# Loading the V cache of a two-layer decode kernel in transfers of four slots

## The chip, the cores and the metric

The kernel runs on one core of one Trainium2 chip. The metric is the device time in microseconds; each number of the result is a median over several executions. One further execution was recorded by the hardware profiler, and all durations of single operations come from it.

## The reference

Eight sequences (B = 8) of one new token each go through two identical layers: attention over a cache, then a small dense network, each behind a layernorm and added to its input. Both layers read the same K and V caches.

```python
# B=8, D=512, Hq=32, Hkv=8, Sk=8192, Dh=128, F=1792; bf16
def A(x, k_cache, v_cache, wq, wo):          # caches: (B, Hkv, Sk, Dh)
    q = (x @ wq).reshape(B, 1, Hq, Dh).transpose(0, 2, 1, 3)
    k, v = repeat(k_cache, 4, axis=1), repeat(v_cache, 4, axis=1)
    p = softmax(einsum("bhqd,bhkd->bhqk", q, k) * Dh ** -0.5)
    o = einsum("bhqk,bhkd->bhqd", p, v)
    return o.transpose(0, 2, 1, 3).reshape(B, 1, Hq * Dh) @ wo

def Bnet(x, w1, w2):
    return silu(x @ w1) @ w2

for _ in range(2):
    x = x + A(layernorm(x), A_k_cache, A_v_cache, A_wq, A_wo)
    x = x + Bnet(layernorm(x), B_w1, B_w2)
```

A head's K is 8192 rows of 128 numbers, 2 MB, and its V as much. There are 64 pairs of batch and head.

## The kernel before

**Tasks and steps.** A task is one (layer, batch, KV head) with its four query heads; there are 128. A task has four steps (`SPT`), one for each piece of 2048 keys. A piece of K or V is 512 KB: 128 partitions of 4 KB, that is 16 chunks of 128 keys. Step c transposes its piece of K on TensorE (line 551; eight chunks at a time), ScalarE and VectorE copy the transposes back over the piece (lines 560 and 562), and TensorE multiplies them with the queries (line 585). The softmax of a task follows when its four steps are through, and the product with V (line 645) runs `LAG` = 6 steps behind: step c works on the V of step c - 6.

**Slots.** All pieces live in one tile, `arena`, of `NSLOT` = 28 neighbouring slots of 4 KB per partition. A slot is used again and again; each has a semaphore of its own, which a load into it raises when it has landed.

**Kept heads.** Layer 1 reads the same caches as layer 0. Of heads 3 to 7 the transposed K of layer 0 stays in its slots until layer 1 of the same batch has used it (`KEEP` = 20 pieces, one of them parked in PSUM), and three pieces of head 7's V as well (`KEEPV`). The other heads are loaded again for layer 1. `make_tasks` orders the tasks accordingly: for each batch, layer 0's heads 3 to 7, while the kept K fills slot after slot; then four other tasks, whose loads have to do with the few slots left (called a tight passage here); then layer 1's heads 3 to 7, which load V alone and set the kept slots free; and then other tasks with slots to spare, in layer 0 or 1. The dense network and the queries of layer 1 are computed in between, in small parts, by `chain_of`.

**The plan of the loads.** `lay_loads` writes down before the kernel runs which load goes into which slot. Time is counted in half steps. Each wanted piece has a `need` (the half step of its first use) and a `free` (that of its last). The pieces are sorted by need and taken one by one; a piece goes into the slot that is free first. A piece with an even number takes its right-hand neighbour along, in one load of 1 MB into two neighbouring slots, if the later of the two is free `WIDE` = 8 half steps before the need; the second piece then leaves the list. `after` is the half step after which the load may be issued: the last use of what the slots held. SP issues the loads in the order of the list; at half step 2c or 2c + 1 `issue_until` issues all at the head of the list whose `after` has come, and before each `Sync.acquire` (waits on line 88, issues on line 407) makes SP wait for the instruction that last used the slots.

**Layout.** A load of two pieces reads one contiguous run of 8 KB for each partition, so partition p holds other keys than it would with two single loads. K and V of the same keys, in either layer where they meet, must be laid out alike. `plan_loads` sees to it: where some of a pair of pieces (`rows_of`: layer, batch, head and number of the pair) come as a pair and some as singles, all are made single and the plan is laid again. `issue` reads the cache in the layout that the plan has settled on.

Of the kernel before, what the change touches and what calls it, by code (L numbers as in the profile page):

```python
# [15 lines left out]
SPT = 4  # L16
NSLOT = 28
# [4 lines left out]
LAG = 6  # L22
WIDE = 8
AHEAD = 8
LEAD = 1
NTP = 2
NSCP = 2
# [111 lines left out]
def make_tasks(nb, nkv, keep_from):  # L139


    first = int(keep_from)
    a = [[(0, b, g) for g in range(first)] for b in range(nb)]
    kept = [[(0, b, g) for g in range(first, nkv)] for b in range(nb)]
    c = [[(1, b, g) for g in range(first, nkv)] for b in range(nb)]
    d = [[(1, b, g) for g in range(first)] for b in range(nb)]
    ahead = [t for b in range(1, nb) for t in a[b]]
    behind = []
    tasks = a[0] + kept[0]
    na = 0  # L150
    rest = 2 * len(ahead) - nb * WINDOW

    def put(size, must):
        nonlocal na, tasks
        nd = max(0, min(len(behind), size - max(0, must - na)))
        tasks += behind[:nd]
        del behind[:nd]
        tasks += ahead[na:na + size - nd]
        na += len(ahead[na:na + size - nd])

    for b in range(nb):
        if b:
            tasks += kept[b]
        gap = rest * (b + 1) // (nb - 1) - rest * b // (nb - 1) if b + 1 < nb else 0
        due = first * min(b + 1, nb - 1)
        put(WINDOW if b + 1 < nb else len(behind), due - gap)
        tasks += c[b]
        behind += d[b]
        if b + 1 < nb:
            put(gap, due)  # L170
    tasks += behind
    assert na == len(ahead)
    return tasks


def rows_of(d, kept):
    return 0 if (d.g, d.k) in kept else d.layer, d.b, d.g, d.k // 2


def plan_loads(tasks, kept, parked, keptv, nslot, ngran):  # L180

    single = set()
    while True:
        loads, copies = lay_loads(tasks, kept, parked, keptv, nslot, ngran, single)
        double = {rows_of(d, kept) for d in loads if d.n == 2}
        torn = {rows_of(d, kept) for d in loads if d.n == 1} & double
        if not torn:
            return loads, copies, double
        single |= torn


def closing_from(tasks, kept):

    i = len(tasks)
    while tasks[i - 1][0] == 1 and (tasks[i - 1][2], 0) not in kept:
        i -= 1
    return i * SPT


def lay_loads(tasks, kept, parked, keptv, nslot, ngran, single):  # L200

    at = {t: i for i, t in enumerate(tasks)}
    wanted = []
    late = closing_from(tasks, kept)
    for i, (layer, b, g) in enumerate(tasks):
        for k in range(ngran):
            c = i * SPT + k
            if layer == 0 or (g, k) not in kept:
                last = i if layer or (g, k) not in kept - parked else at[(1, b, g)]
                wanted.append(Load("K", layer, b, g, k, -1 if c < AHEAD else 2 * (c - LEAD if c >= late else c), 2 * (last * SPT + k) + 1))  # L210
            elif (g, k) in parked:
                wanted.append(Load("C", layer, b, g, k, 2 * (c - 1), 2 * c + 1))
            if layer == 0 or (g, k) not in keptv:
                last = i if layer or (g, k) not in keptv else at[(1, b, g)]
                wanted.append(Load("V", layer, b, g, k, 2 * (c + LAG), 2 * (last * SPT + k + LAG)))
    wanted.sort(key=lambda d: (d.need, d.kind))
    free = [-2] * nslot
    loads, copies = [], []
    while wanted:
        d = wanted.pop(0)  # L220
        if d.kind == "C":
            d.slot = max((j for j in range(nslot) if free[j] < d.need - 1), key=lambda j: (free[j], j))
            free[d.slot] = d.free
            copies.append(d)
            continue
        mate = None
        if d.k % 2 == 0 and rows_of(d, kept) not in single:
            same = [e for e in wanted if (e.kind, e.layer, e.b, e.g, e.k) == (d.kind, d.layer, d.b, d.g, d.k + 1)]
            mate = same[0] if same else None
            s = min(range(nslot - 1), key=lambda j: (max(free[j], free[j + 1]), j))  # L230
            after = max(free[s], free[s + 1])
            if after > d.need - WIDE or d.need < 0 or len(wanted) == 1:
                mate = None
        if mate:
            wanted.remove(mate)
            d.n, d.slot, d.after = 2, s, after
            free[s], free[s + 1] = d.free, mate.free
        else:
            d.slot = min(range(nslot), key=lambda j: (free[j], j))
            d.after = free[d.slot]  # L240
            free[d.slot] = d.free
        assert d.after < d.need or d.need == -1 and d.after == -2, (d.kind, d.need, d.after)
        loads.append(d)
    return loads, copies
# [18 lines left out]
def _build(ctx, nc, A_x, A_k_cache, A_v_cache, A_wq, A_wo, B_w1, B_w2, out):  # L263
    B, _sq, D = A_x.shape
    _b, HKV, S, _dh = A_k_cache.shape
# [6 lines left out]
    NGRAN = NCH // (GRP * HALVES)  # L272
# [4 lines left out]
    kept = set(order[len(order) - KEEP:])  # L277
    keptv = set(order[len(order) - KEEPV:])
    tasks = make_tasks(B, HKV, (len(order) - KEEP) // NGRAN)
    assert len(tasks) == 2 * B * HKV  # L280
    task_at = {t: i for i, t in enumerate(tasks)}
    parked = set(order[len(order) - PARK:])
    loads, copies, wide = plan_loads(tasks, kept, parked, keptv, NSLOT, NGRAN)
    NC = len(tasks) * SPT

    pe = nc.tensor
# [103 lines left out]
    def r_half(slot, h):  # L390
        return res(f"slot{slot}_{h}")
# [10 lines left out]
    def dma(eng, out_ap, in_ap, counter, reads=(), writes=()):  # L402
        reads = [res(n) if isinstance(n, str) else n for n in reads]
        writes = [res(n) if isinstance(n, str) else n for n in writes]
        syn.acquire(eng, reads, writes)
        tok = counter.next_tok()
        eng.dma_start(out_ap, in_ap).then_inc(counter.sem, 16)  # L407
        syn.release(tok, reads, writes)
        return tok
# [14 lines left out]

    def issue(d):
        cache = A_k_cache if d.kind == "K" else A_v_cache
        if rows_of(d, kept) in wide:
            src = cache[d.b, d.g].rearrange("(j p i c) d -> p j i (c d)", j=NGRAN // 2, p=128, i=2)
            src = src[:, d.k // 2, d.k % 2:d.k % 2 + d.n].rearrange("p i e -> p (i e)")
        else:  # L430
            src = cache[d.b, d.g].rearrange("(k p c) d -> k p (c d)", k=NGRAN, p=128)[d.k]
        dst = ARENA[:, d.slot * SLOT:(d.slot + d.n) * SLOT]
        dma(sp, dst, src, slsem[d.slot],
            writes=[r_half(s, h) for s in range(d.slot, d.slot + d.n) for h in range(HALVES)])
        for i in range(d.n):
            (k_slot if d.kind == "K" else v_slot)[(d.b, d.g, d.k + i)] = d.slot + i

    with nc.Block() as block:

        @block.sync  # L440
        def _(sync_eng):
# [34 lines left out]
            def issue_until(pos):  # L476
                while queue and queue[0].after <= pos:
                    issue(queue.pop(0))
# [17 lines left out]

            for _n in range(AHEAD):
                issue(queue.pop(0))
# [70 lines left out]
            def emit_q(ti):  # L569
                layer, b, g = tasks[ti]  # L570
                if layer == 0:
                    q, rq = QA[:, b, g * REP:(g + 1) * REP], f"QA{b}"
                else:
                    q, rq = QT2[b % 2][:, g * REP:(g + 1) * REP], f"QT2_{b % 2}"
                qb = QB[ti % NQB][:, NGRAN - 1:NGRAN - 1 + REP * NGRAN:NGRAN]
                op(act, lambda: act.copy(qb, q), reads=[rq], writes=[f"QB{ti % NQB}"])
# [359 lines left out]
            for f in ln_stages(XT[0], "XT0", B, opens):  # L936
# [3 lines left out]
               reads=["PT", "yr"], writes=["PT"])  # L940
            for c in range(AHEAD):
                for h in range(HALVES):
# [32 lines left out]
            def scores(c):  # L975
                layer, _b, g, _k = where(c)
                if not step(TILE) and not chain and turn[0] < B and heads[turn[0]] and layer == 0 and g >= first:
                    add_heads(turn[0])
                emit_s(c)

            for c in range(NC + LAG):
                if c < NC:
                    layer, b, g, k = where(c)
                if c and c % SPT == 0 and c < NC:
                    assert layer == 0 or asked[b] >= (g + 1) * REP
                    emit_q(c // SPT)
                ready = c < NC and (c < AHEAD or layer == 1 and (g, k) in kept)
                if ready:
                    scores(c)
                t = c + LEAD if c >= late - LEAD else c  # L990
                if not ready or t >= late:
# [72 lines left out]
```

## Time and profile before

| | |
|---|---|
| median of 3 runs | 1133.17 us (1130.16 to 1137.92) |
| profiled execution | 1138.0 us, of which the span from the first to the last instruction 1136.2 us |
| TensorE: matmuls busy / weight loads busy | 930.5 us (82%) / 699.6 us (62%) |
| VectorE / ScalarE / GpSimd busy | 555.3 / 492.2 / 117.8 us |
| mean granted TensorE clock | 0.933 of full speed |
| read from memory | 452.47 MB, 398 GB/s over the span |
| loads of K and V | 347 of V (141 of two slots), 268 of K (84 of two slots) |
| chain that ended last | DMA 49%, TensorE 33%, VectorE 8%, ScalarE 4% |

The page of the profile divides the span into 40 equal slices of 28.4 us; a digit is the busy share of a slice in tenths, PEclk the clock that was granted to TensorE, GB/s what the 16 DMA engines moved. DMA queue q1 carries the loads that SP issues, q8 the fetching of instructions. In the waits, "SPq L88 <- PE OTp L645" reads: SP's queue, at line 88, waited for TensorE's matmuls of line 645. "PEld" is TensorE's loading of weights, which for line 645 are chunks of V. Three numbers behind a wait are its sum in microseconds, how often, and the longest. In the list of DMA issues the last number is the median time from the issue to the landing, with all that stood ahead of it in the queue.

### The profile page before, as it was taken

How to read it: one execution, taken by the hardware profiler on the slowest of the kernel's cores; microseconds unless marked ns; L12 is line 12 of the kernel's file. 1: busy time of each engine (PE TensorE's matmuls, PEld its weight loads, DVE VectorE, ACT ScalarE, POOL GpSimd, SP SyncE). 2: the span in 40 equal slices, each digit the busy share in tenths (PEclk: the TensorE clock that was granted, in tenths of full speed). 3: DMA queues.
4: the chain of work that ended last, by engine and by line, in shares of the span. 5: the costliest groups of instructions: out<-in, count | busy, mean ns of one | idle time of the engine just before them, and what ended most of it. 6: DMA issues, size and time to landing. Idle time of an engine off the chain costs nothing.

```text
span 1136.2 us, 42713 instructions
## 1 busy us (share of the span) xinstructions
PE 930.5 (82%) x18792; PEld 699.6 (62%) x18792; DVE 555.3 (49%) x1710; ACT 492.2 (43%) x778; POOL 117.8 (10%) x300
## 2 busy tenths in 40 slices
PE   6687888888888788888888888888888887878886
PEld 4366656666576556666566655666566665766565
DVE  6444554456344544446444554445444463445544
ACT  5354424554255424554245433554245442544332
POOL 0000110011100110001100111001100111001100
PEclk9699988999899988999699998999899997999987
DMA  9999999999999999999999999999999999999995
GB/s 377 416 414 414 393 406 419 417 396 404 416 418 412 334 400 419 417 409 383 399 419 412 387 399 420 418 412 397 407 418 414 398 401 413 418 413 376 400 418 221
DMA packets 91805, 455.25 MB, mean 401 GB/s; under 512 B 10204, under 2 KB 10468, under 8 KB 62308
## 3 DMA queue, kind: packets, MB, share of 16 engines
q1 hardware_dynamic: 91604, 452.51, 98.9%
q8 instruction: 148, 2.42, 0.9%
q14 instruction: 37, 0.30, 0.1%
q10 hardware_dynamic: 16, 0.01, 0.0%
HBM read 452.47 MB, written 0.01 MB: 398 GB/s over the span
## 4 chain that ended last, share of the span: by engine, by line
DMA 49%; PE 33%; DVE 8%; ACT 4%; issue 4%; SPq 2%; POOL 0%; POOLq 0%; ACTq 0%; DVEq 0%
DMA arena<-in_A_v_cache_dram 29%; DMA arena<-in_A_k_cache_dram 18%; PE TPp L551 15%; PE SCp L585 8%; DVE arena L562 7%; PE OTp L645 4%; ACT arena L560 3%; PE MISC L760 3%; DMA wq<-in_A_wq_dram 2%; PE TPp L625 2%; SPq L407 2%; ACT P L609 1%; PE KEPTp L551 1%; DVE small L634 0%; PE MISC L732 0%
## 5 line engine op out<-in xcount | busy, mean ns | idle before, releaser
L560 ACT COPY arena<-TPp 128x1024 bf16<-128x1024 bf16 x344 | 348.3, 1013 | 388.8 <-PE TPp L551 385.6
L562 DVE COPY arena<-TPp 128x1024 bf16<-128x1024 bf16 x344 | 238.0, 692 | 335.7 <-PE TPp L551 333.7
L551 PE MATMUL TPp<-ident,arena 128*128 128x128 bf16 x5504 | 378.8, 223 | 25.9 <-DMA arena<-in_A_k_cache_dram 19.5
L551 PEld LDWEIGHTS TPp<-ident,arena 128*128 128x128 bf16 x5504 | 318.4, 100 | 112.5 <-issue 64.2
L645 PE MATMUL OTp<-PT,arena 128*128 128x32 bf16 x8192 | 291.3, 179 | 59.4 <-DMA arena<-in_A_v_cache_dram 54.1
L645 PEld LDWEIGHTS OTp<-PT,arena 128*128 128x128 bf16 x8192 | 251.9, 97 | 133.7 <-DMA arena<-in_A_v_cache_dram 100.7
L585 PE MATMUL SCp<-arena,QB 128*32 128x512 bf16 x2048 | 221.5, 421 | 73.0 <-DVE arena L562 27.2
L609 ACT ACTIVATE P<-SCp,small 128x512 bf16<-128x512 f32 x128 | 88.0, 688 | 205.6 <-DVE small L607 169.3
L596 DVE TENSOR_REDUCE small<-SCp 128x1 f32<-128x512 f32 x128 | 88.4, 691 | 96.2 <-PE SCp L585 95.0
L585 PEld LDWEIGHTS SCp<-arena,QB 128*32 128x32 bf16 x2048 | 60.3, 95 | 115.5 <-ACT arena L560 52.1
L600 POOL PARTITION_ALL_REDUCE small<-small x128 | 47.7, 373 | 576.9 <-DVE small L598 576.9
L617 POOL PARTITION_ALL_REDUCE small<-small x128 | 55.4, 433 | 327.4 <-DVE at L659 147.9
L625 PE MATMUL TPp<-ident,P 128*128 128x128 bf16 x512 | 55.0, 235 | 30.4 <-ACT arena L560 17.4
L625 PEld LDWEIGHTS TPp<-ident,P 128*128 128x128 bf16 x512 | 31.4, 103 | 40.1 <-ACT arena L560 24.1
L629 DVE COPY PT<-TPp 128x256 bf16<-128x256 bf16 x128 | 37.3, 291 | 21.6 <-PE TPp L625 19.9
L615 DVE TENSOR_SCALAR small<-small 128x4 f32<-128x4 f32 x128 | 28.7, 224 | 31.1 <-ACT P L609 30.8
L598 DVE TENSOR_SCALAR small<-small 128x4 f32<-128x4 f32 x128 | 29.4, 230 | 4.5
L773 DVE STREAM_TRANSPOSE MISC<-MISC 128x128 f32<-128x128 f32 (+2 forms) x40 | 22.0, 550 | 18.0 <-PE MISC L760 18.0
L605 DVE TENSOR_TENSOR small<-small 128x4 f32<-128x4 f32 x128 | 20.0, 156 | 20.9 <-POOL small L600 20.9
L609 ACT ACTIVATION_READ_ACCUMULATOR P<-SCp,small 128x1 f32 x128 | 24.7, 193 | 0.0
L760 PE MATMUL MISC<-wo,at 128*32 128x128 bf16 x1024 | 24.6, 221 | 0.0
L560 ACT COPY arena<-KEPTp 128x1024 bf16<-128x1024 bf16 x16 | 16.2, 1012 | 14.3 <-PE KEPTp L551 10.9
(102 smaller groups left out, 331.6 us busy)
## 6 DMA issues: line engine op xcount, KB each, us to landing
arena<-in_A_v_cache_dram SPq DMA_DIRECT2D x141, 1024.0 KB, 19.6
arena<-in_A_v_cache_dram SPq DMA_DIRECT2D x206, 512.0 KB, 7.0
arena<-in_A_k_cache_dram SPq DMA_DIRECT2D x184, 512.0 KB, 9.4
arena<-in_A_k_cache_dram SPq DMA_DIRECT2D x84, 1024.0 KB, 22.0
arena<-in_A_wo_dram SPq DMA_DIRECT2D x8, 512.0 KB, 12.7
wq<-in_A_wq_dram SPq DMA_DIRECT2D x1, 4096.0 KB, 25.3
w<-in_B_w_dram SPq DMA_DIRECT2D x1, 1792.0 KB, 23.3
arena<-in_B_w_dram SPq DMA_DIRECT2D x3, 512.0 KB, 17.3
```

The costliest lines, as they stand in the source:

```text
L551: lambda c=c: pe.transpose(tpv[:, c, :], chunk(slot, h * GRP + c), ident[:, :])
L560: op(act, lambda: act.copy(dst, bank[:, :]), reads=[rt], writes=[r_half(slot, h)])
L562: op(dve, lambda: dve.tensor_copy(dst, bank[:, :]), reads=[rt], writes=[r_half(slot, h)])
L585: lambda t=t: pe.matmul(SCp[bank][t * QR:(t + 1) * QR, :], QB[qn][:, NGRAN - 1 - k:NGRAN - 1 - k + QR], keys[:, t * KB:(t + 1) * KB], star ...
L596: op(dve, lambda: dve.tensor_reduce(mxp[st][:, :], SCp[bank][:, :], AX.X, ALU.max), reads=[f"SC{bank}"], writes=[f"mxp{st}"])
L600: op(pool, lambda: pool.partition_all_reduce(mxa[st][:, :], mxr[st][:, :], 128, bass.bass_isa.ReduceOp.max), reads=[f"mxr{st}"], writes=[f ...
L609: op(act, lambda: act.activation(P[:, :], SCp[bank][:, :], ACT.Exp, bias=nb[st][:, 0:1], scale=SM_SCALE, accum_out=rs[st][:, :]), reads=[f ...
L617: op(pool, lambda: pool.partition_all_reduce(ssa[st][:, :], ssm[st][:, :], 128, bass.bass_isa.ReduceOp.add), reads=[f"ssm{st}"], writes=[f ...
L625: lambda c=c: pe.transpose(tpv[:, c, :], P[:, c * 128:(c + 1) * 128], ident[:, :])
L629: op(dve, lambda: dve.tensor_copy(PT[:, :, :, :], tpv.rearrange("p c (t q) -> p c t q", q=QR)[:, :, :, 0:NGRAN * REP]), reads=[f"TP{tb}"], ...
L645: lambda n=n, cc=cc: pe.matmul(otp, chunk(slot, n), PT[:, cc % CPB, (cc // CPB) % NT, cc // (CPB * NT)::NGRAN].unsqueeze(2).to_broadcast([ ...
L760: lambda t=t, col=col, w=w, start=start, stop=stop: pe.matmul(MISC[t * QR:(t + 1) * QR, 0:math.prod(w.shape[1:])], spread(col), w, start=s ...
```

## The change

A load of V may now fill four neighbouring slots, all four pieces of a head, in one transfer of 2 MB. It is made where four neighbouring slots are free 16 half steps before the need and where the need doesn't fall into the 18 half steps (nine steps, `CALM`) before the end of a layer-0 task of head 7, behind which the tight passage begins (`entries`, `calm`). K still comes in ones or twos. A load of four reads 16 KB in one run for each partition; K of the same rows is then read in that layout too, in pairs of 8 KB out of each 16. Where a single load falls among rows that are joined in twos or fours, `plan_loads` bars that joining and lays the plan again (`barred` takes the place of `single`, `joined` that of `wide`). The plan comes to 585 loads of K and V.

```diff
+CALM = 9
...
-def rows_of(d, kept):
-    return 0 if (d.g, d.k) in kept else d.layer, d.b, d.g, d.k // 2
+def rows_of(d, kept, n):
+    return n, 0 if (d.g, d.k) in kept else d.layer, d.b, d.g, d.k // n
...
-    single = set()
+    barred = set()
     while True:
-        loads, copies = lay_loads(tasks, kept, parked, keptv, nslot, ngran, single)
-        double = {rows_of(d, kept) for d in loads if d.n == 2}
-        torn = {rows_of(d, kept) for d in loads if d.n == 1} & double
+        loads, copies = lay_loads(tasks, kept, parked, keptv, nslot, ngran, barred)
+        torn = set()
+        joined = {rows_of(d, kept, d.n) for d in loads}
+        for d in loads:
+            for n in (2, 4):
+                if d.n == 1 and rows_of(d, kept, n) in joined:
+                    torn.add(rows_of(d, kept, n))
         if not torn:
-            return loads, copies, double
-        single |= torn
+            return loads, copies, joined
+        barred |= torn
...
+    entries = [2 * SPT * (i + 1) for i, (layer, _b, g) in enumerate(tasks) if layer == 0 and g == max(g for g, _k in kept)]
+
+    def calm(need):
+        return all(not 0 < e - need < 2 * CALM for e in entries)
+
...
-        mate = None
-        if d.k % 2 == 0 and rows_of(d, kept) not in single:
-            same = [e for e in wanted if (e.kind, e.layer, e.b, e.g, e.k) == (d.kind, d.layer, d.b, d.g, d.k + 1)]
-            mate = same[0] if same else None
-            s = min(range(nslot - 1), key=lambda j: (max(free[j], free[j + 1]), j))
-            after = max(free[s], free[s + 1])
-            if after > d.need - WIDE or d.need < 0 or len(wanted) == 1:
-                mate = None
-        if mate:
-            wanted.remove(mate)
-            d.n, d.slot, d.after = 2, s, after
-            free[s], free[s + 1] = d.free, mate.free
-        else:
-            d.slot = min(range(nslot), key=lambda j: (free[j], j))
-            d.after = free[d.slot]
-            free[d.slot] = d.free
+        for n, ahead in ((4, 2 * WIDE), (2, WIDE), (1, 0)):
+            if d.k % n or n > 1 and (rows_of(d, kept, n) in barred or d.need < 0) or n > 2 and (d.kind == "K" or not calm(d.need)):
+                continue
+            mates = [d] + [e for e in wanted if (e.kind, e.layer, e.b, e.g) == (d.kind, d.layer, d.b, d.g) and d.k < e.k < d.k + n]
+            s = min(range(nslot - n + 1), key=lambda j: (max(free[j:j + n]), j))
+            after = max(free[s:s + n])
+            if len(mates) == n and (n == 1 or after <= d.need - ahead and len(wanted) >= n):
+                break
+        d.n, d.slot, d.after = n, s, after
+        for i, e in enumerate(mates):
+            free[s + i] = e.free
+            if i:
+                wanted.remove(e)
...
-        if rows_of(d, kept) in wide:
-            src = cache[d.b, d.g].rearrange("(j p i c) d -> p j i (c d)", j=NGRAN // 2, p=128, i=2)
-            src = src[:, d.k // 2, d.k % 2:d.k % 2 + d.n].rearrange("p i e -> p (i e)")
-        else:
-            src = cache[d.b, d.g].rearrange("(k p c) d -> k p (c d)", k=NGRAN, p=128)[d.k]
+        n = max(n for n in (1, 2, 4) if n == 1 or rows_of(d, kept, n) in joined)
+        src = cache[d.b, d.g].rearrange("(j p i c) d -> j p i (c d)", j=NGRAN // n, p=128, i=n)
+        src = src[d.k // n, :, d.k % n:d.k % n + d.n].rearrange("p i e -> p (i e)")
```

## The prediction

> **What bounds the kernel now.** I read the page first, for the share of the DMA engines and the rate in 40 slices.
>
> ```profile
> span 1136.2 us, 42713 instructions
> ...
> PEclk9699988999899988999699998999899997999987
> DMA  9999999999999999999999999999999999999995
> GB/s 377 416 414 414 393 406 419 417 396 404 416 418 412 334 400 419 417 409 383 399 419 412 387 399 420 418 412 397 407 418 414 398 401 413 418 413 376 400 418 221
> ...
> q1 hardware_dynamic: 91604, 452.51, 98.9%
> q8 instruction: 148, 2.42, 0.9%
> ```
>
> The queue of the loads keeps all 16 DMA engines busy for 98.9% of the span. The rate is not flat: about 418 GB/s in some slices, 376 to 400 in others, 334 once. So I asked for the busy time of single stretches: two in which pairs of slots are loaded (191.7 and 979.8), one in which single slots are loaded (229.0), and two around a tight passage behind kept heads (247.2, 382.7). After the engines, a row has the granted clock, the DMA share and GB/s.
>
> ```profile
> 191.70:219.60 27.90, 23.43 (x496) 19.20 (x496) 13.51 (x37) 14.79 (x21) 2.41 (x6) 1.00 1.01 420
> 229.00:247.00 18.00, 15.13 (x312) 12.44 (x308) 8.69 (x23) 9.79 (x14) 1.61 (x4) 1.00 1.02 408
> 247.20:268.10 20.90, 17.86 (x404) 13.84 (x404) 12.48 (x44) 10.04 (x15) 2.81 (x7) 1.00 1.00 384
> 382.70:397.10 14.40, 10.67 (x224) 7.92 (x224) 6.91 (x26) 5.11 (x8) 1.21 (x3) 0.88 0.90 300
> 979.80:1005.00 25.20, 21.46 (x450) 17.10 (x448) 11.91 (x32) 12.72 (x18) 2.04 (x5) 1.00 1.01 417
> ```
>
> Pairs flow at 420 (or 417), singles at 408, and only the tight passages fall below that. The DMA issues on the page say how deep the queue is:
>
> ```profile
> arena<-in_A_v_cache_dram SPq DMA_DIRECT2D x141, 1024.0 KB, 19.6
> arena<-in_A_v_cache_dram SPq DMA_DIRECT2D x206, 512.0 KB, 7.0
> arena<-in_A_k_cache_dram SPq DMA_DIRECT2D x184, 512.0 KB, 9.4
> arena<-in_A_k_cache_dram SPq DMA_DIRECT2D x84, 1024.0 KB, 22.0
> ```
>
> A pair lands some 20 us after its issue although it moves in 2.5: eight transfers' worth stand ahead of it. A single V lands after 7.0, so the reserve in the tight passages is five transfers. Last come the waits of SP and, for 707 to 745, those of TensorE:
>
> ```profile
> SPq L88 <- PE OTp L645: 426.1, 232, 6.8
> SPq L88 <- PE SCp L585: 138.2, 142, 6.9
> ```
> ```profile
> PEld OTp L645 <- DMA arena<-in_A_v_cache_dram: 2.0, 2, 1.2
> ```
>
> SP waits for slots that TensorE has yet to free, with the DMA queue still full behind it; TensorE meets V that is not there twice in 38 us. Both run nearly level: the bytes set the time, and V lands just before it is used.
>
> **What the change does to the plan.** I worked the new rule through the list of wanted pieces. It gives 585 loads of K and V: V 21 fours, 105 pairs and 194 singles, K 87 pairs and 178 singles. Before it was V 141 and 206, K 84 and 184, together 615. So 18 singles and 33 pairs go and 21 fours come, with the same bytes. Only 21 heads get a four: K must come in pairs there, four adjacent slots must be free 8 steps ahead, and the nine steps before the end of a head-7 task are barred. Single loads shift between the batches' head 6, which accounts for the 18.
>
> **Price of the transfers.** A single of 0.524 MB at 408 GB/s takes 1.285 us, a pair of 1.049 MB at 420 takes 2.497. With a fixed part f and v for each 0.524 MB, f + v = 1.285 and f + 2v = 2.497, so v = 1.212 and f = 0.073. No row shows a four; by the same two terms it takes 0.073 + 4 x 1.212 = 4.921 us. Sum: -18 x 1.285 - 33 x 2.497 + 21 x 4.921 = -2.19 us, that is 30 transfers fewer at 0.073. The bounds from the nearest rows: a four without any fixed part (4.848) makes it -3.7, a four at four singles (5.140) makes it +2.4. I keep 4.921, since rows of 4 KB to 8 KB already follow the two terms and the four merely doubles the row to 16 KB. With 417 GB/s for pairs f is 0.055 and the sum -1.7.
>
> The Trainium skill (DMA: Bandwidth & Descriptors, section Anatomy of one DMA) gives a DMA about 2.0 us of fixed time, mostly until its completion is confirmed; by that 30 fewer would be worth 60 us. The stretches disagree: 0.073 us is what a transfer adds while the queue is full.
>
> **What waits longer.** A load is one completion. A four's first half lands with its second, 2 x 1.25 = 2.5 us later than the pair did, and K pairs that stood between the two V pairs move back by the same. The trace's landings, matched with the first matmul on line 645 that reads each, say how much room there is: the pairs that fours replace landed 0.05 to 5.3 us before their use, 17 of 21 less than 2.5 us. So TensorE will wait there, up to 2.5 us less the room. The lateness doesn't add up within one batch's run of fours, for the next four finds the use as late as the last one made it. The largest in each of the eight runs are 2.4, 0.8, 2.0, 1.0, 2.4, 2.4, 2.4, 2.4: 16 us, if all of it stayed.
>
> I expect it not to stay. A layer-0 task takes TensorE 9.2 us at full clock (tasks come every 9.2 us between 191.7 and 228.5), while its 4.19 MB take DMA 10.0 us at 420 GB/s. A TensorE that is late finds data waiting and is again at the data's pace after three tasks. The barred nine steps are 2.25 tasks, which gives back 2.25 x 0.8 = 1.8 us; at most 0.65 is left of 2.45, eight times 5.2 us, and the tight passage meets even that with some 7 us of queued transfers. I take 0, and 5.2 as the upper end.
>
> **What SP waits for.** A four is issued when the last of its four slots is free, and behind it in SP's order stand the next K pairs and V. Counted in pieces asked for but not yet used, the new plan has 13 or more (16 us at 1.25 each) around the issue of 20 of the 21 fours, and 8 at the one of batch 5's head 6 in layer 1, where the old plan has 6; in the steps behind the kept heads it has the same 5 as before. So DMA doesn't run dry. The 30 issues less are hidden: SP stands waiting for slots for over 560 us. At the entry to the layer-1 kept heads the least reserve falls from 7 to 5 in two batches and rises from 5 or 6 to 7 in three, through the head-6 shifts; I set that at zero, and at about 1 us either way. The end is unchanged: the last task still ends on single V pieces.
>
> **The rivals.**
> 1. *The lateness stays (slower).* TensorE leaves a run of fours late, frees its slots late, and in the tight passage, where the reserve is five slots, DMA stands still for as long. For it: that passage already runs at 384 and 300 instead of 408, and the chain of waits runs through TensorE's transposes from 190 to 252 and then through a V load issued there. Against it: the 0.8 us a task that a late TensorE wins back. Price +16 - 2.2: 1147. It decides once the waits for V in the runs are not won back by the first single-slot task.
> 2. *A 16 KB row is dear (slower).* The only packets of that size are those of q8: 0.9% of 16 engines' 1136.2 us over 148 packets is 1.1 us each, against 0.6 us for an eighth of 4.921. At 1.1 a four takes 8.8 us and the sum is about +80: 1213. Against it: q8's packets share each engine with a queue that is busy 98.9% of the time, so their time is mostly turns taken.
> 3. *The tight passages heal (faster).* All cache loads at clean rates are 390 x 1.285 + 225 x 2.497 = 1063 us, the 12 MB of weights 29.5; some 44 us remain for start, end and tight passages. A quarter of it, 11 us, would be 1120. Only the better entries speak for it.
> 4. *Each transfer costs its completion (faster).* The first load, with nothing ahead of it, landed 3.8 us after its issue by the trace, 2.5 more than its 1.285; 30 x 2.5 is 75 us, 1058. A queue eight transfers deep covers that. This is the rule of the Trainium skill named above.
>
> **How the numbers follow.** The profiled execution took 1138.0 us (span 1136.2 and 1.8 around it), 4.8 over the median of the three runs, 1133.17. Less 2.2 it would be 1135.8; against the median 1131. The forecast has 0.86, rivals 1 to 4 have 0.08, 0.02, 0.03 and 0.01. Within the forecast: below, no fixed part at all (-1.5) and the runs' own spread (-3.0) give 1126; above, the rest of the lateness (5.2) and the spread (4.8) give 1141, which also holds a four at the price of singles. That range leaves out the rivals' 0.14 and little of the forecast. About 1% (11.3 us) is what a measurement here can tell from no change; forecast and its range lie inside, so within 1% has 0.86, slower 0.10, faster 0.04.
>
> **What would show it.** Right: 21 issues of 2048 KB for V; pair stretches at 420 to 424 GB/s; the passage behind kept heads at its old 384 or so; waits of L645 for V up to 2.5 us in the runs of fours and none more in the single-slot tasks; a span 1 to 4 us shorter at the same clock. Wrong: slices below 410 where the fours flow (rival 2); tight slices slower than before by some 2 us each (rival 1); or tight slices at 400 and above (rival 3). A throttled clock in another passage than before, as at 382.7 now, would blur all this by a few us.

## The result, and the profile after

| | median | range | executions |
|---|---|---|---|
| before | 1131.47 us | 1127.73 to 1137.92 | 18 |
| after | 1140.26 us | 1133.20 to 1145.86 | 18 |

The change makes the kernel slower: the ratio of after to before is 1.0071, with a 95% interval of 1.0054 to 1.0088, some 8 us. The forecast was 2 us faster; the time lies inside the predicted range, the direction is wrong.

A warning comes before the profiles. The profiled execution of the kernel after took 1133.2 us, the fastest of its 18; that of before took 1138.0, as much as the highest of its 18. Set side by side, these two profiles say that the change gains 5 us. What single operations cost can be read from them, the total can't. I therefore took a second profile of each and judged everything else by timed runs.

The page of the kernel after, in the lines that answer to those of the prediction:

```profile
span 1131.4 us, 42643 instructions
...
PEclk9699988999899988999789988999889996999987
DMA  9999999999999999999999999999999999999995
GB/s 376 416 420 412 389 401 419 417 401 402 417 418 405 369 409 419 421 410 390 417 422 415 390 407 419 423 411 388 406 420 417 371 403 420 421 414 384 410 420 204
...
q1 hardware_dynamic: 87284, 452.51, 98.8%
...
arena<-in_A_v_cache_dram SPq DMA_DIRECT2D x105, 1024.0 KB, 11.9
arena<-in_A_v_cache_dram SPq DMA_DIRECT2D x194, 512.0 KB, 6.5
arena<-in_A_k_cache_dram SPq DMA_DIRECT2D x178, 512.0 KB, 8.1
arena<-in_A_k_cache_dram SPq DMA_DIRECT2D x87, 1024.0 KB, 21.3
arena<-in_A_v_cache_dram SPq DMA_DIRECT2D x21, 2048.0 KB, 23.2
```

There are 21 loads of 2048 KB, the DMA engines are as full as before (98.8% against 98.9%), and slices with fours reach 420 to 423 GB/s. Over the stretch of single-slot loads, over the tight passage behind it, and over a stretch in which fours flow, the busy times of the kernel after are (clock, DMA share and GB/s at the end of a row):

```profile
229.00:247.00 18.00, 14.92 (x303) 12.15 (x300) 8.58 (x24) 9.43 (x15) 1.50 (x4) 1.00 1.02 406
247.20:268.10 20.90, 17.78 (x417) 14.17 (x413) 12.93 (x44) 10.66 (x16) 3.13 (x8) 1.00 1.00 389
...
965.00:995.00 30.00, 24.41 (x507) 19.78 (x508) 13.85 (x39) 15.58 (x24) 2.40 (x6) 1.00 1.01 422
```

The bandwidth is as forecast: 422 GB/s where fours flow, and the two others run at 406 and 389, about as before (408 and 384). What is new stands in TensorE's weight loads. This is the timeline of that queue in the kernel after, lines in which it waited for a DMA, in two stretches (start, duration, and in brackets the idle time before it and what ended it; line 650 is the line 645 of before):

```profile
340.59 0.47 PEld L650 LDWEIGHTS OTp<-PT,arena 128*128 128x128 bf16 x16 [2.72 <-DMA arena<-in_A_v_cache_dram]
```
```profile
825.75 0.50 PEld L650 LDWEIGHTS OTp<-PT,arena 128*128 128x128 bf16 x16 [3.24 <-DMA arena<-in_A_v_cache_dram]
...
828.23 1.62 PEld L556 LDWEIGHTS TPp<-ident,arena 128*128 128x128 bf16 x16 [0.89 <-DMA arena<-in_A_k_cache_dram]
```

Before, TensorE's weight loads waited for no DMA at all in the first of these places (334.5 to 344), and the waits for V around the second were 0.4 to 1.4 us. The kernel before has at the second place:

```profile
828.34 0.47 PEld L645 LDWEIGHTS OTp<-PT,arena 128*128 128x128 bf16 x16 [0.81 <-DMA arena<-in_A_v_cache_dram]
...
830.85 1.62 PEld L551 LDWEIGHTS TPp<-ident,arena 128*128 128x128 bf16 x16 [1.20 <-DMA arena<-in_A_k_cache_dram]
```

The first wait has a sequel, seen in the next window of the same kernel:

```profile
341.00:344.40 3.40, 3.38 (x59) 2.72 (x55) 0.41 (x1) 1.11 (x2) 0.00 (x0) 0.50 1.03 420
```

The granted clock is 0.50 for 3.4 us directly after the 2.7 us of waiting, in a stretch that runs at 1.00 before the change. The task, from its first score matmul to that of the next, lost 3.6 us (12.85 instead of 9.21), not 2.7.

### The profile page after: what moved, and what is told of

The parts are those of the page before. It is cut to its first block, busy times and chain, and to the rows that moved or that the text cites. A ratio compares the mean times of both kernels' runs of the same rounds, so it can differ in the third digit from the quotient of the medians.

```text
span 1131.4 us, 42643 instructions
## 1 busy us (share of the span) xinstructions
PE 923.4 (82%) x18792; PEld 702.5 (62%) x18792; DVE 555.0 (49%) x1710; ACT 492.0 (43%) x778; POOL 117.3 (10%) x300
## 3 DMA queue, kind: packets, MB, share of 16 engines
q1 hardware_dynamic: 87284, 452.51, 98.8%
## 4 chain that ended last, share of the span: by engine, by line
PE 39%; DMA 39%; DVE 10%; ACT 5%; issue 5%; SPq 1%; POOL 0%; POOLq 0%; ACTq 0%; DVEq 0%
DMA arena<-in_A_v_cache_dram 30%; PE TPp L556 19%; PE SCp L590 10%; DVE arena L567 8%; DMA arena<-in_A_k_cache_dram 6%; ACT arena L565 4%; PE OTp L650 4%; PE MISC L765 3%; PE TPp L630 2%; DMA wq<-in_A_wq_dram 2%; SPq L414 1%; PE KEPTp L556 1%; ACT P L614 1%; DVE small L639 0%; DVE small L610 0%
## 5 line engine op out<-in xcount | busy, mean ns | idle before, releaser
L612 DVE TENSOR_REDUCE small<-small 128x1 f32<-128x4 f32 x128 | 20.1, 157 | 4.4
```

## The experiments

All ratios are to the kernel before, run beside each kernel on the same chip, with 95% intervals. In the short diffs `loads` is the list that SP issues in order.

**The changed kernel again, and its fours as halves.** A four differs from two pairs in three things: it lands as a whole (theory L), its second half stands ahead of K and V that are needed sooner (theory O), and it waits until all four slots are free, with everything behind it in SP's queue (theory W). Besides, the new plan uses other slots and shifts head 6 (theory S). Two kernels keep the changed plan, its slots and its layout of the rows, and issue each four as two pairs.

```diff
# halves_together: the second pair right behind the first, both when the four slots are free
+        if d.n == 4:
+            e = Load(d.kind, d.layer, d.b, d.g, d.k + 2, d.need + 4, d.free + 4)
+            e.n, e.slot, e.after = 2, d.slot + 2, d.after
+            d.n = 2
+            out += [d, e]
# halves_apart: each when its own two slots are free, the second in the place of its own need
+            d.after, e.after = d.each
...
+    return sorted(out, key=lambda d: (d.need, d.kind))
```

> The changed kernel once more, timed beside the others and profiled again, since its first profile (1133.2 us) was its fastest execution and that of the kernel before (1138.0) its slowest. Theory L (a four lands as a whole, so its first half lands 2.5 us later than the pair it replaces, and TensorE carries the lateness into the passages behind the kept heads): about 1139 to 1141, and at the head of each tight passage tasks that start up to 2.5 us later than before. Theory S (the slots, the shifts of head 6 and the entry reserve of the new plan are what costs): the same total, with the loss at the entries to the kept heads of layer 1 in the batches whose least reserve fell from 7 to 5.

> The kernel before, only for a second profile: about 1131 us. Both theories expect tasks of 9.2 us in the pair stretches and the loss in the tight passages; it shows how much of one profile's differences is mere spread.

> The changed plan, slots, order and layout, but each four is issued as two pairs, one right behind the other, each with its own completion. Theory L: the first half lands 2.5 us sooner, the loss goes: about 1131 to 1133. Theory O (the second half's bytes stand ahead of K that is needed sooner): stays at 1138 to 1140. Theory S: stays at 1139 to 1141. A price of the 16 KB rows would also go here: 1131 to 1133.

> The changed plan's slots and layout, but each four is issued as two pairs, each waiting for its own two slots alone, the second in the place of its own need. Theory L and theory O: about the time before, 1130 to 1133. Theory S: 1139 to 1141.

Measured: after_again 1.0057 (1.0030 to 1.0084), halves_together 1.0045 (1.0024 to 1.0067), halves_apart 0.9987 (0.9969 to 1.0006); the second profile of before was one execution of 1136.13 us. Theory S falls: the new slots and the shifts of head 6 cost nothing that can be seen once each half stands in its own place. Theory L explains at most the small rest between 1.0045 and 1.0057 to 1.0071, whose intervals overlap. The 16 KB rows are no cause either: the two kernels of halves read the same 16 KB spans in runs of 8 KB, and one of them is slow.

**Order or slots.** The next two kernels cross the two remaining differences.

```diff
# wait_four: own places, but both halves wait for all four slots
+            e.after = d.after
...
+    return sorted(out, key=lambda d: (d.need, d.kind))
# early_own: the second half right behind the first, each waits for its own two slots
+            d.after, e.after = d.each
...
+    return out
```

> Two pairs in place of each four, the second in the place of its own need, as in halves_apart (0.9987 of the time before), but both wait until all four slots are free, as the four does. Theory W (SP's wait for four free slots, with the K behind it in SP's order, is what costs): back at 1.004 to 1.006. Theory O (the second half's bytes stand ahead of K and of the next V): stays at 0.998 to 1.001.

> Two pairs in place of each four, the second right behind the first, as in halves_together (1.0045), but each waits for its own two slots alone. Theory O: stays at 1.003 to 1.006, since the order of the bytes is the same. Theory W, if it is the first half's wait alone: 0.998 to 1.001; if the wait of the second half, which still blocks SP's queue at the same place, is what counts, it can't be told from theory O here, and wait_four decides.

Measured: wait_four 0.9985 (0.9962 to 1.0009), early_own 1.0042 (1.0017 to 1.0066). The wait for four free slots costs nothing that can be seen; the order of the bytes costs about 0.0055, six of some 8 us. In early_own V's first half lands as early as a pair's, and yet TensorE is as late as in the kernel after: it is K that comes late. Here is the same place as above in early_own, behind the last V of the layer-1 kept heads of batch 5 (line 572 is the transposing of K):

```profile
822.33 0.47 PEld L666 LDWEIGHTS OTp<-PT,arena 128*128 128x128 bf16 x16 [0.81 <-DMA arena<-in_A_v_cache_dram]
...
827.29 1.62 PEld L572 LDWEIGHTS TPp<-ident,arena 128*128 128x128 bf16 x16 [3.66 <-DMA arena<-in_A_k_cache_dram]
```

and in halves_apart:

```profile
822.38 0.47 PEld L666 LDWEIGHTS OTp<-PT,arena 128*128 128x128 bf16 x16 [0.81 <-DMA arena<-in_A_v_cache_dram]
...
824.86 1.42 PEld L572 LDWEIGHTS TPp<-ident,arena 128*128 128x128 bf16 x16 [1.19 <-DMA arena<-in_A_k_cache_dram]
827.38 0.50 PEld L666 LDWEIGHTS OTp<-PT,arena 128*128 128x128 bf16 x16 [1.09 <-DMA arena<-in_A_v_cache_dram]
```

The V ahead lands at the same moment; K of head 2 of batch 6 comes 2.4 us later in early_own, about the 2.5 us of the 1 MB that was put in front of it. halves_apart then waits 1.09 us for the second half of V, which early_own already has; its next transposing begins at 828.46 all the same, that of early_own at 830.61, so 2.2 us stay.

**Where it is not won back.** Measured from the first score matmul of a task to that of the next, task 93, layer 1's head 7 of batch 5, took 8.9 to 9.2 us in the profiles without an early second half there (before, before_again, halves_apart, wait_four) and 11.3 in those with one (after, after_again, halves_together, early_own). The last three tasks took 38.6 to 39.9 us without and 39.7 to 42.1 with one. Two kernels take these two fours apart from the rest.

```diff
# two_apart: halves in their own places for these two heads alone
+        if d.n == 4 and (d.layer, d.b, d.g) in ((1, 5, 6), (1, 7, 0)):
# two_whole: for all other heads
+        if d.n == 4 and (d.layer, d.b, d.g) not in ((1, 5, 6), (1, 7, 0)):
```

> The changed kernel, but the fours of the two heads in whose places all three profiles with early second halves were longer, (1,5,6) (stretch of tasks 89 to 95: 41.5 to 41.9 us against 38.8 to 40.1) and (1,7,0) (tasks 120 to 128: 70.7 to 71.7 against 69.4 to 69.7 before), are issued as halves in their own places. Theory P (these two places carry most of the loss, because TensorE has no time there to win it back): 1.001 to 1.003 instead of 1.006. Theory A (the loss is spread over all fours): 1.005 to 1.006.

> The reverse: only the fours of (1,5,6) and (1,7,0) are whole, the 19 others are issued as halves in their own places. Theory P: 1.002 to 1.004 (halves_apart had 0.9987). Theory A: 0.999 to 1.000.

Measured: two_apart 1.0024 (1.0003 to 1.0045), two_whole 1.0031 (1.0004 to 1.0057). Over halves_apart the two fours alone cost 0.0044, the other 19 together 0.0037, and the sum, 0.0081 or 9 us, is about what the whole change costs over halves_apart (0.0070 to 0.0084). Theory P holds for about half: two of 21 fours carry about as much as the rest, as far as intervals of 0.002 to 0.003 either way can tell. Each of the two by itself, and four others with room:

```diff
# only_156, only_170, roomy: whole are (1,5,6) alone; (1,7,0) alone; four heads with room
+        if d.n == 4 and (d.layer, d.b, d.g) != (1, 5, 6):
...
+        if d.n == 4 and (d.layer, d.b, d.g) != (1, 7, 0):
...
+        if d.n == 4 and (d.layer, d.b, d.g) not in ((0, 0, 2), (1, 2, 0), (0, 3, 3), (0, 6, 2)):
```

> Of the 21 fours only that of (1,5,6) is whole, 20 are issued as halves in their own places (halves_apart had 0.9987; two_whole, with this and the next, 1.0031). In every profile with an early second half there, TensorE came to K of the next task 2.2 us later (task 93: 11.3 us instead of 8.7 to 9.2). Theory P (what is lost there stays): 1.000 to 1.002. If it is won back later: 0.998 to 1.000.

> Of the 21 fours only that of (1,7,0), the last, is whole. The stretch of the last three tasks took 39.7 to 42.1 us with an early second half there and 38.6 (once 39.9) without, and nothing follows in which it could be won back. Theory P: 1.000 to 1.002, about 2 us over halves_apart.

> Only the four fours whose replaced pairs had landed 2.3 us or more before their use are whole: (0,0,2), (1,2,0), (0,3,3), (0,6,2). If a four costs only where the room is less than the 2.5 us by which it moves others back: 0.998 to 1.000, as halves_apart. If each four costs its share of the rest (some 0.003 over 19 fours): 0.999.

Measured: only_156 1.0013 (0.9989 to 1.0036), only_170 1.0002 (0.9977 to 1.0026), roomy 0.9980 (0.9965 to 0.9995). Each of the first two lies above halves_apart, by 0.0026 and 0.0015, but within the intervals; timed alone, neither is settled. Their profiles show the same lateness as the kernel after: task 93 takes 11.33 us in only_156 and 8.71 in only_170, the last three tasks 41.3 in only_170. The four fours of roomy cost nothing that can be seen: its ratio is the lowest of the study and the only one whose interval lies below the kernel before, by 0.2%; from halves_apart (0.9987) it is not told apart.

They were picked by the room of V, and by that measure the four of (1,7,0) belongs to them: its pair had landed 2.8 us before its use (2.4 in the second profile). What sets them apart is the room of the pair of K behind which the second half of V stood. The same matching of landings with first uses, for that K in the two profiles of the kernel before, gives 3.0 to 6.5 us for the four heads of roomy, but 0.05 us at (1,5,6) and 1.5 and 1.1 us at (1,7,0). (In halves_apart it is 1.4 us at (0,0,2), 2.7 to 4.8 us at the three others, and 0.05 and 1.2 us at the two.) No run picks fours by this measure.

The end shows why nothing there comes back. In the chain that ended last, the kernel after has, near its end:

```profile
1083.81 22.50 DMA arena<-in_A_k_cache_dram
1106.31 0.05 issue
1106.35 1.07 PE TPp L556 x16
```

K of the last task, behind the last four, lands at 1106.3; from there on the chain is TensorE's and what follows it. In halves_apart TensorE's weight loads wait for no DMA between 1095 and 1112, and its chain runs through TensorE from 1088.6 on:

```profile
1073.48 15.06 DMA arena<-in_A_k_cache_dram
1088.59 1.89 PE TPp L572 x16
```

**Order alone, in the old kernel.** The last experiment has no four and no new plan. It swaps neighbours in the old list.

```diff
+    for i in range(len(loads) - 1):
+        d, e = loads[i], loads[i + 1]
+        if (d.kind, d.n, e.kind, e.n) == ("K", 2, "V", 2) and d.need == e.need:
+            loads[i], loads[i + 1] = e, d
```

> The kernel before, with its own plan and slots and no four, but at 58 places the V pair is issued ahead of the K pair of the same half step, so 1 MB stands ahead of K as it does behind a four. In two profiles 22 and 31 of these K pairs landed less than 2.5 us before their use. Theory O (bytes needed later that stand ahead of K make TensorE late): slower, 1.003 to 1.010. If order alone cost nothing and only the new plan did: 0.998 to 1.001.

Measured: 1.0056 (1.0032 to 1.0081). The same bytes in the same slots, with 1 MB of V ahead of K at 58 places, cost about as much as the whole change with its 21. In 57 of the 58 the slots of V come free after those of K, so K is also issued later; but at the three places below K still landed 15 to 17 us after its issue, so what made it late is what stood ahead of it in the queue. These are the longest waits of TensorE's weight loads for K or V in v_first, at the first K behind layer 1's kept heads (line 555), in three batches alike:

```profile
181.25 1.62 PEld L555 LDWEIGHTS TPp<-ident,arena 128*128 128x128 bf16 x16 [3.37 <-DMA arena<-in_A_k_cache_dram]
```
```profile
309.35 1.49 PEld L555 LDWEIGHTS TPp<-ident,arena 128*128 128x128 bf16 x16 [3.42 <-DMA arena<-in_A_k_cache_dram]
```
```profile
435.81 1.62 PEld L555 LDWEIGHTS TPp<-ident,arena 128*128 128x128 bf16 x16 [3.90 <-DMA arena<-in_A_k_cache_dram]
```

The kernel before waited 0.9 us for each of the three (0.7 to 1.4 us in its second profile), as here for the second:

```profile
302.82 0.90 PEld L551 LDWEIGHTS TPp<-ident,arena 128*128 128x128 bf16 x16 [0.89 <-DMA arena<-in_A_k_cache_dram]
```

## Why the prediction was wrong

**The plan and the price of the transfers: right.** The 585 loads are those that were counted, and a four moves as fast as the two terms said: 0.073 + 4 x 1.212 = 4.92 us was the estimate, and the packets of 16 KB in the trace take 613 ns at the median, eight of them 4.90 us. (That the rows of 4 and 8 KB follow the two terms was no support, since the terms were worked out from these two; the 16 KB are the first test.) Rival 2, a dear row of 16 KB, is out.

**What SP waits for: right.** The wait for four slots was set at nothing. wait_four, which keeps it and changes only the order, is at 0.9985.

**What waits longer: the mechanism right, its cover wrong.** The prediction has the step that costs: a four lets V's first half land 2.5 us later and moves the K that stood between the two pairs of V back by as much, 17 of the 21 pairs of V have less room than that, and the lateness sums to 16 us if it all stays. It then said "I expect it not to stay" and took 0, with 5.2 us as the upper end. That is the step that failed. The measured term is 8 to 9.5 us over the same plan with the halves in their own places, between the 5.2 and the 16. That 1140.26 still lies within the range is luck: the upper end adds 4.8 us for the spread of three runs to the 5.2, and the kernel is 8.8 us over the median of the one before. Missing in the step were:

- It measured the room of V alone. The runs show that it is K that comes late: early_own brings V's first half as early as a pair, and is slow all the same. By the room of V the last four, of (1,7,0), cost nothing; the K behind it had 1.5 us of room.
- It counted tasks of 9.2 us against 10.0 us of DMA everywhere. That holds in the layer-0 stretches, and in them some of the lateness is indeed won back: behind the wait at 340 the next two tight tasks of the kernel after run at 9.21 us where they took 10.43 and 10.12 before (9.21 and 9.83 in the second profile). But the four of (1,5,6) lies at the exit of the kept heads of layer 1, where TensorE meets its data with 0.05 us of room, and the barred nine steps are laid before the entry to a tight passage, not there. With that of (1,7,0) it costs 0.0044, about half of the loss.
- "The end is unchanged" was wrong. The last four pushes K of the last task back, and behind that no transfer is left whose wait could shrink.
- Some waits cost more than their length: behind the one at 340.6 the clock stood at 0.50 for 3.4 us, and the task lost 3.6 us with 2.7 of waiting. The prediction knew low clocks only as a blur. How much of the 8 us this makes stays open.

**Rival 1: the direction right, its price too high, its place not borne out.** It had the lateness carried into the tight passages and lost there. The tight passages behind layer 0's kept heads, all eight together, take 305.3 to 318.9 us in the four profiles with an early second half (after, after_again, halves_together, early_own) and 311.3 to 317.2 in four without (before, before_again, halves_apart, wait_four): no loss is seen there. The eight stretches of the kept heads themselves, where most fours lie, take 379.1 to 386.1 us with and 375.8 to 380.1 without. How the loss divides over the stages is not to be read from single profiles: after_again against halves_apart would put 10.3 us into these stretches and leave nothing for the two fours outside them, to which the timed runs give half of the loss.

Rivals 3 and 4 are out with the direction. The 2.0 us of the Trainium skill (DMA: Bandwidth & Descriptors, Anatomy of one DMA) that the prediction set beside rival 4 stand there for transfers that GpSimd issues; the loads here are SP's.

## What to carry to other kernels

Where a full DMA queue is served in order (here the 615 loads of K and V before and the 585 after all landed in the order of their issue) and data lands just before its use, the price of a larger transfer is not its own time but the bytes in it that are needed later: each stands in front of something needed sooner. Compare, for every load that moves back, its room (landing to first use) with the time of those bytes, and grant nothing as won back at the end of the program or at the exit of a stage in which the compute engine waits for data anyway. Take the room of what is pushed back, here K, not only that of the joined load. Where it was larger, as in roomy, joined transfers cost nothing that could be seen; they gained nothing clear over halves_apart either.

## What the runs showed of the hardware that was not expected

A TensorE wait of about 2 to 3 us can be followed by 3.4 us at half clock: after 2.72 us at 340.6 in the kernel after, after 2.90 us at 215.9 in after_again (clock low from 217.1), after 2.10 us at 743.1 in two_apart (clock low from 744.8):

```profile
743.09 0.47 PEld L666 LDWEIGHTS OTp<-PT,arena 128*128 128x128 bf16 x16 [2.10 <-DMA arena<-in_A_v_cache_dram]
```
```profile
744.80:748.20 3.40, 2.95 (x41) 2.44 (x39) 1.61 (x3) 1.34 (x3) 0.14 (x1) 0.50 1.02 422
```

The Trainium skill (TensorE: Matmul & The Clock Gate, Part 1: The HAM clock gate) says that the clock falls to half after an idle window of about 3.4 us, and that these windows run free. The length of the low stretches, 3.4 us and multiples, agrees; the waits here are shorter than such a window and the clock fell all the same.

The length of one wait does not decide it. In before_again a wait of 2.29 us that ended at 94.4 was followed by 3.4 us at 1.00, while the clock was at 0.50 from 287.7 on behind 3.4 us in which no wait of TensorE's weight loads was over 0.7 us. What share of the 8 us is clock and what is the wait itself was not separated. The mean clock over all executions is 0.930 to 0.934 in the five kernels that put V ahead of K throughout (after, after_again, halves_together, early_own, v_first) and 0.936 to 0.939 in halves_apart, wait_four and the kernel before beside them. The clock may so have a part in the loss; how large, and whether as a cause, is open.

A single profiled execution was off by up to 8.4 us from its kernel's median (1146.89 against 1138.49 in halves_together; 1133.2 against 1140.26 in the kernel after), as much as the whole effect. Among the 18 executions of the kernel after, the seven with a mean clock of 0.926 or less took 1142.2 us on average, the eleven others 1138.4.
